# PSUM banks for layer-one sums and transposed rows, the place of the transposes, and a search level of ten VectorE operations

## The chip, the core and the metric

The kernel runs on one core of a Trainium2 chip. Times are device microseconds of the whole program. Before the change three runs took 708.53, 710.94 and 711.21 us, median 710.94. A separate execution, recorded by the hardware profiler, took 707.02 us; its span from the first to the last instruction is 705.3 us.

In what follows PE is TensorE, PEld its weight load, DVE is VectorE, ACT ScalarE, POOL GpSimd and SP the engine that issues most transfers.

## What is computed

Two stages. First a retention attention: for 8 batches, 8 heads, 576 positions and 64 features, scores times a decay mask times v. Its output is 4608 tokens of 512 features. Then a mixture of 8 experts, in which each expert takes exactly 576 tokens:

```python
logits = x @ w_gate                     # 4608 x 8
for idx in np.argsort(-logits.flatten()):
    tok, e = idx // 8, idx % 8
    if assigned[tok] >= 0 or counts[e] >= 576: continue
    assigned[tok] = e; counts[e] += 1
for e in range(8):
    out[assigned == e] = np.maximum(x[assigned == e] @ w1[e], 0) @ w2[e]   # 512 -> 1024 -> 512
```

The greedy assignment is not done token by token: the kernel searches for the score at which the next expert becomes full, removes that expert and its tokens, and searches again.

## The kernel before

The attention fills about the first 180 us; the search for the first expert to fill runs to about 215 us. From there the experts run one after the other on PE, in the order in which they fill, called e = 0 to 7 here. For each, five indirect transfers on POOL (`gather`, L949) fetch its tokens into `xg`. `transposes` (L954 to 970) turns them on PE in five pieces j = 0 to 4, four of 128 tokens and one of 64, each into one PSUM bank `pt`; ACT copies the bank to `xh` (the rounded high part) and DVE subtracts to get `xl` (the low part). `l1` (L972) forms 16 sums `ph`, one for each of eight blocks f of 128 hidden features and each of two token groups s (256 and 320 tokens): 12 matmuls into one bank, then ACT's ReLU into `hb` (L997) and DVE's low part of it (L1000). Both read the bank and thereby free it. `l2` (L1015) forms five sums `py` for five token pieces t, 24 matmuls for t = 0 to 3 and 16 for t = 4; ACT (for t = 4 also DVE, L1052) moves each to `yt`, and POOL scatters it to the output (L1009). `conv` (L923) splits a loaded weight piece `raw` into high and low parts with two ACT copies and a POOL accumulating transfer.

PSUM's eight banks are named by tag: "t" and "r" have one each, "y", "h0" and "h1" two each. A tag's buffers are taken in rotation, and an instruction that takes a buffer waits until its last readers are done. Before, `ph` with s = 0 always took "h0" and with s = 1 "h1", so a sum had to wait for the readers of the sum two blocks earlier. `py` has "y". The five pieces of a transpose took t, h0, h1, t, h0 for e of 1 and above, and t, y, y, t, y for e = 0. Everything of the search uses "r".

While PE works for expert e, DVE searches for a later expert (`search`, L285): seven levels. In a level DVE compares every token's candidate digit with K candidates (`reach`, L161, output `G`), PE counts with nine small matmuls into bank r (L312), and DVE turns the 32 x 8 counts into a digit `j` by twelve operations (L315 to L329). From it come `v` (L297), the next `G`, and `u` (L307). After the levels come `members` (PE at L383), `listing` (PE at L421 and L424) and `leave`, which takes the found expert out of the scores (`best`) and prepares the next search.

Every engine executes its instructions in the order in which the program emitted them. That order comes from a planner, `Mixer` (L854). It keeps an estimated PE time `t` and DVE time `v`; each matmul group of `l1` or `l2` advances `t` (`mix.adv`), and DVE work beside the search advances `v` (`mix.vec`). The search is a generator that yields an estimated DVE duration and PE duration; its next piece is emitted when `t` reaches the time at which the estimate says it is ready. A gather notes when its rows will have come, as `t` plus a constant (`arrives`, L952), and the transposes begin at the first slot of `l2` after that, one piece a slot. The estimates are constants in the code and know nothing of real waits.

Of the kernel before, what the change touches and what calls it, by code (L numbers as in the profile page):

```python
# [10 lines left out]
F32 = mybir.dt.float32  # L11
# [3 lines left out]
ALU = mybir.AluOpType  # L15
AF = mybir.ActivationFunctionType
AX = mybir.AxisListType
# [46 lines left out]
def widths(shifts):  # L64
    return [1 << (a - b) for a, b in zip([32] + shifts[:-1], shifts)]
# [16 lines left out]
class Route:  # L82
# [202 lines left out]
    def search(s):  # L285
        nc, V, pool, ps = s.nc, s.nc.vector, s.pool, s.ps
        SH, KK = LATER, widths(LATER)
        for _ in s.ordered():
            pass
        s.dig(0)  # L290
        for it, K in enumerate(KK):
            last = it == len(SH) - 1
            v2 = pool.tile([128, 36, 2], BF16, name="v", bufs=2)
            v = v2[:, :, 0]
            if it:

                V.tensor_scalar(v2, u[:, :, None].to_broadcast([128, 36, 2]), j, None, op0=ALU.subtract)  # L297
            else:
                V.tensor_copy(v2, s.dg[:, 0, :, None].to_broadcast([128, 36, 2]))
            s.reach(0, 36, K, v2, ALU.is_le)  # L300
            if it == 0:
                for k in range(1, 7):
                    s.dig(k)
                V.tensor_copy(s.D[:, 1:], s.dg[:, 1:])
            if not last:
                u = pool.tile([128, 36], F32, name="u")
                V.scalar_tensor_tensor(u, v, float(KK[it+1]), s.D[:, it+1], op0=ALU.mult, op1=ALU.add)  # L307

            yield (2050 + 19*K if it else 1350), 310
            cp = ps.tile([128, 32], F32, name="r")  # L310
            for c in range(0, 36, 4):
                nc.tensor.matmul(cp, s.G[:, c:c+4].rearrange("p c k -> p (c k)"), s.oh[:, c:c+4, :], start=(c == 0), stop=(c == 32))  # L312
            own = [cp[32*c:32*c+32, 8*c:8*c+8] for c in range(4)]
            cs, ct = pool.tile([32, 8], F32, name="cs"), pool.tile([32, 8], F32, name="ct4")
            V.tensor_tensor(cs, own[0], s.nr[:32], op=ALU.add)  # L315
            V.tensor_copy(ct, own[1])
            V.tensor_tensor(cs, own[2], cs, op=ALU.add)
            V.tensor_tensor(ct, own[3], ct, op=ALU.add)
            V.tensor_tensor(cs, cs, ct, op=ALU.add)
            if last:  # L320
                break

            mc, mq = pool.tile([32, 1], F32, name="mc"), pool.tile([128, 1], F32, name="mq")
            tc, j = pool.tile([128, 32], F32, name="tc"), pool.tile([128, 1], F32, name="j")
            V.tensor_reduce(mc, cs, axis=AX.X, op=ALU.max)
            for q in range(0, 128, 32):
                V.tensor_scalar(mq[q:q+32], mc, 0.0, float(KK[it+1]), op0=ALU.is_ge, op1=ALU.mult)  # L327
            V.transpose(tc, mq.to_broadcast([128, 32]))
            V.tensor_reduce(j, tc[:, 1:K], axis=AX.X, op=ALU.add)  # L329

        for q in range(0, 128, 32):
            V.tensor_scalar(s.f[q:q+32, :8], cs, 0.0, None, op0=ALU.is_ge)
        tf, cf = pool.tile([128, 32], F32, name="tc"), pool.tile([128, 32], F32, name="cf")
        nk, nf = pool.tile([128, 1], F32, name="nk"), pool.tile([128, 1], F32, name="nf")
        w = pool.tile([128, 8], F32, name="w8")
        s.ge = pool.tile([128, 2, 36], F32, name="ge")
        s.gt, s.eq = s.ge[:, 0], s.ge[:, 1]
        V.transpose(tf, s.f)
        V.tensor_reduce(nk, tf[:, :K], axis=AX.X, op=ALU.add)
        V.transpose(cf, nk.to_broadcast([128, 32]))  # L340
        V.tensor_reduce(nf, cf[:, :8], axis=AX.X, op=ALU.max)
        V.scalar_tensor_tensor(w, cf[:, :8], nf, s.dec, op0=ALU.is_equal, op1=ALU.mult)
        V.tensor_scalar(s.gt, v, nf, -1.0, op0=ALU.subtract, op1=ALU.is_gt)
        V.tensor_scalar(s.eq, v, nf, -1.0, op0=ALU.subtract, op1=ALU.is_equal)
        s.pick(w)
# [539 lines left out]
def moe(tc, nc, P, R, xd, w1_d, w2_d, out, mix):  # L885
    V, A, T = nc.vector, nc.scalar, nc.tensor
# [4 lines left out]
    state = dict(dma=0, conv=0, most=2, listing=-1)  # L891
# [51 lines left out]
    def gather(e):  # L943
        if e in XG or not ready(e):
            return
        xg = P["c"].tile([128, 5, DM], F32, name="xg", tag="xg")
        for j in range(5):
            n = 128 if j < 4 else 64
            nc.gpsimd.indirect_dma_start(out=xg[:n, j, :], out_offset=None, in_=xd[:, :],  # L949
                                         in_offset=bass.IndirectOffsetOnAxis(ap=found[e][:n, j:j+1], axis=0))  # L950
        XG[e] = xg
        state['arrives'] = mix.t + 7000  # L952

    def transposes(e):  # L954

        xg = XG[e]
        xh = P['w'].tile([128, 4, 576], F32R, name="xh", bufs=1)
        xl = P['w'].tile([128, 4, 576], F32R, name="xl", bufs=1)
        XH[e], XL[e] = xh, xl
        for j in range(5):  # L960
            n = 128 if j < 4 else 64
            tag = ("t", "h0", "h1")[j % 3] if e else ("t", "y", "y")[j % 3]
            pt = P['ps'].tile([128, 4, 128], F32R, name="pt", tag=tag, bufs=1 + (tag != "t"))
            for d in range(4):
                T.transpose(pt[:, d, :n], xg[:n, j, d*128:(d+1)*128].bitcast(F32R), P['ident_r'][:n, :n])  # L965
            o, l = [x[:, :, j*128:j*128+n] for x in (xh, xl)]
            A.activation(o, pt[:, :, :n].bitcast(F32), AF.Copy)
            V.tensor_tensor(l, pt[:, :, :n].bitcast(F32), o.bitcast(F32), op=ALU.subtract)
            mix.vec(610)
            yield  # L970

    def l1(e, tr):  # L972
# [5 lines left out]
        for i, (f, s) in enumerate(order):  # L978
# [6 lines left out]
                    pass  # L985
            xh, xl = XH[e], XL[e]
            c, n = ((slice(0, 256), 256), (slice(256, 576), 320))[s]
            ps = P['ps'].tile([128, n], F32, name="ph", tag=f"h{s}", bufs=2)
            terms = [(w[:, d], x[:, d, c]) for d in range(4) for w, x in ((wh, xh), (wh, xl), (wl, xh))]
            if e == 0 and f < 2:  # L990
                terms = terms[0::3] + terms[2::3] + terms[1::3]
# [6 lines left out]
            for a, b in ((0, 256),) if s == 0 else ((0, 256), (256, 320)):  # L998
                to = (640 if a == 0 else 64) + 256*s
                V.scalar_tensor_tensor(hb[:, f, to+a:to+b], ps[:, a:b], 0.0, hb[:, f, 256*s+a:256*s+b].bitcast(F32),  # L1000
                                       op0=ALU.max, op1=ALU.subtract)
# [13 lines left out]
    def l2(e, hb):  # L1015
# [42 lines left out]
        if e + 1 < E and e + 1 not in XH:  # L1058
            mix.drain(lambda: ready(e + 1))
            gather(e + 1)  # L1060
            tr = transposes(e + 1)
# [88 lines left out]
```

## Time and profile before

| What | Value |
|---|---|
| Runs | 708.53, 710.94, 711.21 us; median 710.94 |
| Profiled execution | 707.02 us, its span 705.3 us |
| Mean granted PE clock | 0.984 |
| PE busy over the span | 664.8 us, 94% |
| DVE, ACT, POOL busy | 434.5, 315.5, 182.8 us |
| 228 to 545 us (experts, with searches) | PE busy 300.14 of 317 us, DVE 256.82 |
| 545 to 672 us (experts, no search left) | PE busy 127.00 of 127 us, DVE 30.61 |

The profiled execution lies 3.9 us under the median of the runs. An instruction's row shows its start, its duration, and in brackets how long its engine had stood idle before it and whose end ended that. Matmuls overlap: one row is longer than the distance to the next, so idle time in front of a matmul is counted from the modelled end of the one before, and is a little less than what the stream lost.

### The profile page before, as it was taken

What the parts mean: (1) busy time and instruction counts of PE and PEld (TensorE: products, weight loads), DVE (VectorE), ACT (ScalarE), POOL (GpSimd) and SP (SyncE); (2) the same over time, 40 slices, a digit from 0 to 9 for tenths busy, and PEclk for the clock granted to TensorE, in tenths of its full rate; (3) what the DMA queues carried; (4) which work ended last, traced back from release to release, by engine and by line L of the source; (5) the groups of instructions that cost most, each with busy time, mean ns of one, the idle gap of its engine ahead of it and who ended that gap; (6) DMA issues with size and microseconds to landing.
All of it is one profiled execution on the core that took longest, in us unless ns stands there. A gap on an engine that the chain in (4) does not pass through costs nothing.

```text
span 705.3 us, 14450 instructions
## 1 busy us (share of the span) xinstructions
PE 664.8 (94%) x5462; PEld 579.3 (82%) x5464; DVE 434.5 (62%) x1656; ACT 315.5 (45%) x551; POOL 182.8 (26%) x236
## 2 busy tenths in 40 slices
PE   5999999999899989999999998999999999999995
PEld 5998988879684877798688778778978988988984
DVE  4466766857846588989688788769977321321200
ACT  2655555545311733455345514633551671571511
POOL 3222211121203211614314314124123233232111
PEclk9999999999959999999999999999999999999999
DMA  7986688785316664987938946884794796895421
GB/s 226 348 303 232 218 275 304 244 278 155 101 66 232 146 152 131 229 214 227 253 90 227 227 126 168 205 208 125 179 229 135 184 220 199 204 219 176 90 60 37
DMA packets 53429, 134.74 MB, mean 191 GB/s; under 512 B 6128, under 2 KB 22512, under 8 KB 53360
## 3 DMA queue, kind: packets, MB, share of 16 engines
q1 hardware_dynamic: 38400, 81.91, 34.6%
q0 software_dynamic: 14960, 51.91, 33.2%
q8 instruction: 43, 0.70, 0.4%
q14 instruction: 26, 0.21, 0.1%
HBM read 81.90 MB, written 18.87 MB: 143 GB/s over the span
## 4 chain that ended last, share of the span: by engine, by line
PE 59%; DVE 20%; DMA 8%; issue 6%; ACT 3%; SPq 1%; POOL 1%; POOLq 0%; DVEq 0%; ACTq 0%
PE py L1032 20%; PE ph L993 15%; PE pA L577 7%; PE pX L628 4%; DMA raw<-in_w 3%; PE pS L593 3%; PE pX L618 3%; DVE hb L1000 2%; DVE G L161 2%; PE pt L965 1%; DVE mq L327 1%; PE r L270 1%; DMA vin<-in_vk 1%; PE pT L657 1%; DMA w1l<-raw 1%
## 5 line engine op out<-in xcount | busy, mean ns | idle before, releaser
L1032 PE MATMUL py<-w2h,hb 128*128 128x512 f32 x576 | 189.1, 401 | 0.0
L993 PE MATMUL ph<-xh,w1h 128*128 128x320 f32 (+1 forms) x512 | 152.6, 302 | 4.7 <-DVE hb L1000 2.5
L993 PE MATMUL ph<-xh,w1l 128*128 128x320 f32 (+1 forms) x512 | 149.6, 296 | 0.5 <-DMA w1l<-raw 0.5
L993 PE MATMUL ph<-xl,w1h 128*128 128x320 f32 (+1 forms) x512 | 149.5, 296 | 0.0
L1032 PE MATMUL py<-w2l,hb 128*128 128x512 f32 (+1 forms) x320 | 125.8, 393 | 0.0
L1032 PEld LDWEIGHTS py<-w2h,hb 128*128 128x128 f32 x576 | 104.6, 189 | 21.1
L993 PEld LDWEIGHTS ph<-xh,w1h 128*128 128x128 f32 x512 | 96.3, 189 | 6.8 <-ACT w2l L937 2.6
L997 ACT ACTIVATE hb<-ph 128x256 fp32r<-128x256 f32 (+1 forms) x128 | 52.0, 408 | 109.8 <-PE ph L993 107.6
L993 PEld LDWEIGHTS ph<-xh,w1l 128*128 128x128 f32 x512 | 96.3, 189 | 0.7 <-DMA w1l<-raw 0.7
L993 PEld LDWEIGHTS ph<-xl,w1h 128*128 128x128 f32 x512 | 96.5, 190 | 0.3
L1000 DVE SCALAR_TENSOR_TENSOR hb<-ph,hb 128x256 fp32r<-128x256 f32 (+1 forms) x192 | 58.8, 352 | 54.7 <-ACT hb L997 54.1
L577 PE MATMUL pA<-qin,kz 128*128 128x128 f32 x576 | 75.5, 287 | 7.2 <-DMA qin<-in_qk 5.8
L599 ACT ACTIVATE S<-pS,cst 64x128 f32<-64x128 f32 x128 | 46.4, 362 | 76.5 <-PE pS L593 74.9
L577 PEld LDWEIGHTS pA<-qin,kz 128*128 128x128 f32 x576 | 70.3, 200 | 9.7 <-ACT kz L518 7.6
L1009 POOL DMA_INDIRECT out_y<-yt,idx x40 | 40.3, 1008 | 114.4 <-ACT yt L1049 75.7
L1032 PEld LDWEIGHTS py<-w2l,hb 128*128 128x128 f32 (+1 forms) x320 | 57.0, 178 | 13.3 <-DMA w2l<-raw 0.2
L559 POOL TENSOR_TENSOR ks<-nin,cst 128x512 f32<-128x512 f32 (+1 forms) x33 | 33.4, 1028 | 131.1 <-DMA nin<-in_vk 67.9
L1049 ACT ACTIVATE yt<-py 128x512 f32<-128x512 f32 x32 | 19.1, 598 | 104.1 <-PE py L1032 81.4
L581 DVE TENSOR_TENSOR am<-pA,cst 128x512 f32<-128x512 f32 (+1 forms) x80 | 48.3, 633 | 24.1 <-PE pA L577 23.8
L938 POOL DMA_DIRECT2D w2l<-raw x32 | 28.8, 899 | 127.3 <-ACT hb L997 127.3
L949 POOL DMA_INDIRECT xg<-xd,idx x40 | 41.0, 1025 | 67.6 <-issue 30.0
L1052 DVE TENSOR_TENSOR yt<-yt,py 64x512 f32<-64x512 f32 x8 | 5.4, 680 | 69.7 <-ACT yt L1051 69.6
(179 smaller groups left out, 985.6 us busy)
## 6 DMA issues: line engine op xcount, KB each, us to landing
raw<-in_w SPq DMA_DIRECT2D x64, 512.0 KB, 5.2
w2l<-raw POOLq DMA_DIRECT2D x32, 512.0 KB, 5.1
w1l<-raw POOLq DMA_DIRECT2D x31, 512.0 KB, 6.0
kin<-in_qk SPq DMA_DIRECT2D x14, 576.0 KB, 6.5
qin<-in_qk SPq DMA_DIRECT2D x14, 576.0 KB, 7.0
vin<-in_vk SPq DMA_DIRECT2D x14, 576.0 KB, 5.7
nin<-in_vk SPq DMA_DIRECT2D x14, 512.0 KB, 5.3
xd<-xr SPq DMA_DIRECT2D x36, 192.0 KB, 3.1
```

The lines of the kernel that those rows point to most:

```text
L559: nc.gpsimd.tensor_tensor(KS[u][:, a:b], LD[u, 'n'].rearrange("p (a d) -> p a d", d=64)[:, a:b], ks[:, u % HP, a:b, None].to_broadcast([12 ...
L577: nc.tensor.matmul(pa[:, j, h], KZ[u % 2][:, h, s], LD[u, 'q'][:, s], start=True, stop=True)
L581: nc.vector.tensor_tensor(am[:, :n], pa[:, :n], m[:, None, 2*hp:2*hp+2, :].to_broadcast([128, n, 2, 128]), op=ALU.mult)
L599: nc.scalar.activation(st[64*h:64*h+64, :, 64*h:64*h+64], PS[u][64*h:64*h+64], AF.Copy, scale=ss[64*h:64*h+64, hp, c:c+1])
L628: nc.tensor.matmul(px[64*h:64*h+64, :], v[:, blk*128+64*h:blk*128+64*h+64], AM[g][:, h, :], start=False, stop=blk < 8, skip_group_check=True)
L938: nc.gpsimd.dma_start(lo, raw, accum_op=ALU.add)
L949: nc.gpsimd.indirect_dma_start(out=xg[:n, j, :], out_offset=None, in_=xd[:, :], in_offset=bass.IndirectOffsetOnAxis(ap=found[e][:n, j:j+1] ...
L993: T.matmul(ps, w, x, start=(k == 0), stop=(k == 11))
L997: A.activation(hb[:, f, c], ps, AF.Relu)
L1000: V.scalar_tensor_tensor(hb[:, f, to+a:to+b], ps[:, a:b], 0.0, hb[:, f, 256*s+a:256*s+b].bitcast(F32), op0=ALU.max, op1=ALU.subtract)
L1009: st = nc.gpsimd.indirect_dma_start(out=out[:, :], out_offset=bass.IndirectOffsetOnAxis(ap=found[e][:n, t:t+1], axis=0), in_=y[:n], in_off ...
L1032: T.matmul(ps[:m], a, w, start=(k == 0), stop=(k == last), skip_group_check=True)
```

## The change

Line numbers here are those of the kernel before; in the changed kernel they are one or two lower or higher in these functions.

- `l1`: the sums of the blocks f = 2 and f = 5 take their bank from "y" and no longer from h0 or h1.
- `transposes`: for e of 1 and above the pieces take t, h0, h1, h0, h1. For e = 0 the list is spelled out and is the same as before.
- `gather`: `arrives` is the planned time plus 9000 in place of 7000.
- `search`: the counts are summed with reversed sign by three operations in a row, the last of the four count blocks is compared with that sum in four operations that write the 128 x 8 array `f` directly, and one reduction over `f` takes the place of the reduction and the four 32 x 1 comparisons. The factor K moves from there into `v` (a second operation of the same instruction), and `D` is divided by K once for each search so that `u` is a plain sum. The planner's numbers for a level are kept.

```diff
-                V.tensor_scalar(v2, u[:, :, None].to_broadcast([128, 36, 2]), j, None, op0=ALU.subtract)
+                V.tensor_scalar(v2, u[:, :, None].to_broadcast([128, 36, 2]), j, float(K), op0=ALU.subtract, op1=ALU.mult)
...
-                V.tensor_copy(s.D[:, 1:], s.dg[:, 1:])
+                for a, b in ((1, 4), (4, 7)):
+                    V.tensor_scalar(s.D[:, a:b], s.dg[:, a:b], 1.0/KK[a], None, op0=ALU.mult)
...
-                V.scalar_tensor_tensor(u, v, float(KK[it+1]), s.D[:, it+1], op0=ALU.mult, op1=ALU.add)
+                V.tensor_tensor(u, v, s.D[:, it+1], op=ALU.add)
...
-            cs, ct = pool.tile([32, 8], F32, name="cs"), pool.tile([32, 8], F32, name="ct4")
-            V.tensor_tensor(cs, own[0], s.nr[:32], op=ALU.add)
-            V.tensor_copy(ct, own[1])
-            V.tensor_tensor(cs, own[2], cs, op=ALU.add)
-            V.tensor_tensor(ct, own[3], ct, op=ALU.add)
-            V.tensor_tensor(cs, cs, ct, op=ALU.add)
+            cs = pool.tile([32, 8], F32, name="cs")
+            V.scalar_tensor_tensor(cs, s.nr[:32], -1.0, own[0], op0=ALU.mult, op1=ALU.subtract)
+            for x in own[1:3]:
+                V.tensor_tensor(cs, cs, x, op=ALU.subtract)
+            for q in range(0, 128, 32):
+                V.tensor_tensor(s.f[q:q+32, :8], own[3], cs, op=ALU.is_ge)
...
-            V.tensor_reduce(mc, cs, axis=AX.X, op=ALU.max)
-            for q in range(0, 128, 32):
-                V.tensor_scalar(mq[q:q+32], mc, 0.0, float(KK[it+1]), op0=ALU.is_ge, op1=ALU.mult)
+            V.tensor_reduce(mq, s.f[:, :8], axis=AX.X, op=ALU.max)
...
-        for q in range(0, 128, 32):
-            V.tensor_scalar(s.f[q:q+32, :8], cs, 0.0, None, op0=ALU.is_ge)
...
-        state['arrives'] = mix.t + 7000
+        state['arrives'] = mix.t + 9000
...
-            tag = ("t", "h0", "h1")[j % 3] if e else ("t", "y", "y")[j % 3]
+            tag = ("t", "h0", "h1", "h0", "h1")[j] if e else ("t", "y", "y", "t", "y")[j]
...
-            ps = P['ps'].tile([128, n], F32, name="ph", tag=f"h{s}", bufs=2)
+            ps = P['ps'].tile([128, n], F32, name="ph", tag="y" if f in (2, 5) else f"h{s}", bufs=2)
```

How the rows move on the engines is shown at three places. Everything up to the first search level inside `l1` of e = 0 stands as before on PE, and POOL's rows are the same throughout.

DVE, one level of the search in `l1` of e = 0 (`cs`, `ct`, `mc`, `mq`, `tc`, `j` are the small tiles between the counts `r` and the digit `j`). Before:

```order
L315 TENSOR_TENSOR cs<-r,room 32x8
L316 COPY ct_2952<-r 32x8
L317 TENSOR_TENSOR cs<-r,cs 32x8
L318 TENSOR_TENSOR ct_2952<-r,ct_2952 32x8
L319 TENSOR_TENSOR cs<-cs,ct_2952 32x8
L325 TENSOR_REDUCE mc<-cs 32x1
L327 TENSOR_SCALAR mq<-mc 32x1 x4
L328 STREAM_TRANSPOSE tc<-mq 128x32
L329 TENSOR_REDUCE j<-tc 128x1
L297 TENSOR_SCALAR v<-u,j 128x72
L161 TENSOR_TENSOR G<-ct,v 128x1152
L307 SCALAR_TENSOR_TENSOR u<-v,D 128x36
```

Now:

```order
L317 SCALAR_TENSOR_TENSOR cs<-room,r 32x8
L319 TENSOR_TENSOR cs<-cs,r 32x8 x2
L321 TENSOR_TENSOR f<-r,cs 32x8 x4
L327 TENSOR_REDUCE mq<-f 128x1
L328 STREAM_TRANSPOSE tc<-mq 128x32
L329 TENSOR_REDUCE j<-tc 128x1
L297 TENSOR_SCALAR v<-u,j 128x72
L161 TENSOR_TENSOR G<-ct,v 128x1152
L308 TENSOR_TENSOR u<-v,D 128x36
```

Twelve operations between the counts and `j` have become ten, and seven of them instead of four read the counts' bank.

ACT, from the third `yt` of e = 0's `l2` to the first ReLU of e = 1's `l1` (`w1h`, `w1l` are a `conv`, `xh` the transposed pieces). Before:

```order
L1049 ACTIVATE yt<-py 128x512
L967 ACTIVATE xh<-pt 128x4x128
L933 ACTIVATE w1h<-raw 128x1024
L937 ACTIVATE w1l<-raw 128x1024
L967 ACTIVATE xh<-pt 128x4x128 x3
L1049 ACTIVATE yt<-py 128x512
L967 ACTIVATE xh<-pt 128x4x64
L933 ACTIVATE w1h<-raw 128x1024
L937 ACTIVATE w1l<-raw 128x1024
L1051 ACTIVATE yt<-py 64x512
L997 ACTIVATE hb<-ph 128x256
```

Now:

```order
L1048 ACTIVATE yt<-py 128x512
L931 ACTIVATE w1h<-raw 128x1024
L935 ACTIVATE w1l<-raw 128x1024
L965 ACTIVATE xh<-pt 128x4x128
L1048 ACTIVATE yt<-py 128x512
L965 ACTIVATE xh<-pt 128x4x128 x3
L931 ACTIVATE w1h<-raw 128x1024
L935 ACTIVATE w1l<-raw 128x1024
L965 ACTIVATE xh<-pt 128x4x64
L1050 ACTIVATE yt<-py 64x512
L996 ACTIVATE hb<-ph 128x256
```

Four of the five pieces now stand behind the fourth `yt`, and the last one behind the fourth `conv` as well.

PE, in the same `l2` after the first nine small matmuls of a search. Before:

```order
L1032 MATMUL py<-w2h,hb 128x512 x2
L1032 MATMUL py<-w2l,hb 128x512
L1032 MATMUL py<-w2h,hb 128x512 x2
L1032 MATMUL py<-w2l,hb 128x512
L965 MATMUL pt<-ident,xg 128x128 x4
L1032 MATMUL py<-w2h,hb 128x512 x2
L1032 MATMUL py<-w2l,hb 128x512
L965 MATMUL pt<-ident,xg 128x128 x4
```

Now:

```order
L1031 MATMUL py<-w2l,hb 128x512
L1031 MATMUL py<-w2h,hb 128x512 x2
L1031 MATMUL py<-w2l,hb 128x512
L963 MATMUL pt<-ident,xg 128x128 x4
L1031 MATMUL py<-w2h,hb 128x512
L1031 MATMUL py<-w2l,hb 64x512
L313 LDWEIGHTS G
L313 MATMUL r<-oh,G 128x32
```

The first piece stands after 15 `py` matmuls instead of 6, at the end of t = 3, and the other four within t = 4.

In `l2` of e = 1 the first piece stands behind 51 instead of 42 matmuls of `py`, in e = 2 behind 6 instead of 3; from e = 3 on it stands behind the first three, as before. The search's groups shift a little with them. Between L424 and the first group of L312 of the next search there now stand 66 matmuls of `ph` in e = 2, 63 in e = 3, and 54 with 2 of `py` in e = 4, where there stood 54 with 6 of `py` and 4 of `pt`, 69, and 63. On SP one weight load has changed places with the load of an expert's number.

More of the change, by code (lines that the diff above doesn't have):

```diff
@@ L313, in search @@
             own = [cp[32*c:32*c+32, 8*c:8*c+8] for c in range(4)]
-            cs, ct = pool.tile([32, 8], F32, name="cs"), pool.tile([32, 8], F32, name="ct4")
[L315 to L319, printed above, removed]
+            cs = pool.tile([32, 8], F32, name="cs")
[4 more added lines that the diff above has]
+                V.tensor_tensor(s.f[q:q+32, :8], own[3], cs, op=ALU.is_ge)
             if last:
                 break
-            mc, mq = pool.tile([32, 1], F32, name="mc"), pool.tile([128, 1], F32, name="mq")
+            mq = pool.tile([128, 1], F32, name="mq")
             tc, j = pool.tile([128, 32], F32, name="tc"), pool.tile([128, 1], F32, name="j")
-            V.tensor_reduce(mc, cs, axis=AX.X, op=ALU.max)
-            for q in range(0, 128, 32):
-                V.tensor_scalar(mq[q:q+32], mc, 0.0, float(KK[it+1]), op0=ALU.is_ge, op1=ALU.mult)
+            V.tensor_reduce(mq, s.f[:, :8], axis=AX.X, op=ALU.max)
             V.transpose(tc, mq.to_broadcast([128, 32]))
             V.tensor_reduce(j, tc[:, 1:K], axis=AX.X, op=ALU.add)
-        for q in range(0, 128, 32):
-            V.tensor_scalar(s.f[q:q+32, :8], cs, 0.0, None, op0=ALU.is_ge)
         tf, cf = pool.tile([128, 32], F32, name="tc"), pool.tile([128, 32], F32, name="cf")
```

## Prediction

> **What bounds the kernel now.** I read the stages first, then PE's waits in the stage that has them, then the single waits in the order of time.
>
> The stages (from the view by windows; columns: stretch, its length, busy us and instructions of PE, PEld, DVE, ACT, POOL, then PE clock, DMA share, GB/s):
>
> ```profile
> core 0: us, PE busy (x) PEld busy (x) DVE busy (x) ACT busy (x) POOL busy (x), PEclk, DMA share, GB/s
> 228.00:545.00 317.00, 300.14 (x2135) 259.30 (x2134) 256.82 (x1142) 142.35 (x223) 92.91 (x120) 0.99 0.71 182
> 545.00:672.00 127.00, 127.00 (x803) 115.95 (x802) 30.61 (x88) 65.42 (x104) 35.20 (x49) 1.00 0.73 182
> ```
>
> Once no search is left (545 to 672 us) PE is never idle. While searches run beside the experts it is idle for 16.9 of 317 us, at full clock and with the transfers at the same 0.7 share in both. What differs is DVE: 257 us busy against 31. The diff leaves the attention and the search for the first expert as they are. So the question is which of these 16.9 us go. The view of waits, PE alone, 228 to 545 us (us in total, times, longest):
>
> ```profile
> PE r L312 <- DVE G L161: 5.8, 8, 2.0
> PE pt L965 <- DVE xl L968: 4.1, 4, 1.7
> PE ph L993 <- DVE hb L1000: 2.5, 3, 1.1
> PE ph L993 <- ACT hb L997: 1.2, 1, 1.2
> PE r L383 <- DVE sc L374: 0.9, 1, 0.9
> PE ph L993 <- ACT xh L967: 0.9, 1, 0.9
> PE ph L993 <- DMA w1l<-raw: 0.5, 1, 0.5
> PE r L421 <- DVE rh L415: 0.5, 1, 0.5
> ```
>
> They add to 16.4 us. The 0.9 on xh and the 0.5 on w1l are the first expert's start, which the diff does not touch. 15.0 us are left, of three kinds: banks that DVE or ACT free late (4.1 + 2.5 + 1.2 = 7.8), search levels that DVE finishes late (5.8), and the two steps after the search (1.4). The largest ones, from the timeline of PE (start, us, idle before and whose end it waited for):
>
> ```profile
> 250.24 0.39 PE L312 MATMUL r<-oh,G 128*128 128x32 bf16 x9 [1.95 <-DVE G L161]
> 284.05 0.39 PE L312 MATMUL r<-oh,G 128*128 128x32 bf16 x9 [1.16 <-DVE G L161]
> 336.04 0.40 PE L1032 MATMUL py<-w2l,hb 128*128 128x512 f32 x1
> 338.18 0.54 PE L965 MATMUL pt<-ident,xg 128*128 128x128 f32 x4 [1.74 <-DVE xl L968]
> 382.87 0.38 PE L993 MATMUL ph<-xh,w1h 128*128 128x320 f32 x1 [1.09 <-DVE hb L1000]
> 414.51 0.39 PE L312 MATMUL r<-oh,G 128*128 128x32 bf16 x9 [0.68 <-DVE G L161]
> 425.33 0.38 PE L993 MATMUL ph<-xh,w1h 128*128 128x320 f32 x1 [1.20 <-ACT hb L997]
> 433.83 0.39 PE L993 MATMUL ph<-xh,w1h 128*128 128x320 f32 x1 [1.09 <-DVE hb L1000]
> ```
>
> And the normal pace, from the chain of waits:
>
> ```profile
> 544.93 20.99 PE ph L993 x156
> 571.29 22.29 PE py L1032 x97
> ```
>
> So a ph matmul takes 20.99/156 = 0.135 us and a py matmul 22.29/97 = 0.23. At 338.18 the start lies 2.14 us behind the one before, 1.91 more than 0.23, while the row says 1.74 idle: each wait costs the stream about 0.17 us beyond its row.
>
> **The change, part by part.**
>
> **Transposed rows (4.1 us).** At 338.18 the fourth piece wants bank t, which the first piece holds until DVE's subtraction; DVE does a whole search level first. With five different banks no piece waits for another. The two h0 and two h1 banks were last read for the blocks f = 6 and 7, one expert's l1 earlier; the pieces come at least 3 py matmuls apart, and DVE's reads of those blocks run ahead of the xl work in its queue. I take all 4.1; the bound on the other side is that the last piece waits for f = 7's readers, and half comes back.
>
> **Banks of the first layer (3.7 us).** A sum's bank came free when the readers of the sum two blocks earlier were done. With f = 2 and 5 in y every bank comes back after three blocks: one block is 24 matmuls, 24 x 0.135 = 3.2 us more cover, against waits of 1.2 at most. All 3.7 go. Part returns, since PE now reaches the next search sooner and DVE does not. The case after 425.33, from PE's and DVE's timelines:
>
> ```profile
> 426.96 0.17 PE L424 MATMUL r<-n,ones 128*128 128x8 bf16 x1
> 435.62 0.76 DVE L161 TENSOR_TENSOR G<-ct,v 128x1152 bf16<-128x1152 bf16 x1
> 437.55 0.39 PE L312 MATMUL r<-oh,G 128*128 128x32 bf16 x9
> ```
>
> DVE's G ends at 436.38, 9.4 us behind L424. PE now has 63 ph matmuls between the two, 63 x 0.135 + 0.2 = 8.7 us: a new wait of 0.7. In e = 2 the 66 matmuls (9.1 us) give 0.3 by the same 9.4. In e = 4 PE had 63 matmuls (8.7 us) and no wait in the list; with 54 ph and 2 py (7.9 us) and less hb work for DVE I estimate 0.3. That is 1.3 us against the 7.8; the ends are 0 and 3.7.
>
> **Search levels.** From the groups of instructions (busy us, mean ns of one | idle before):
>
> ```profile
> L315 DVE TENSOR_TENSOR cs<-r,room 32x8 f32<-32x8 f32 x42 | 6.2, 147 | 20.6 <-PE r L312 20.5
> L316 DVE COPY ct<-r 32x8 f32<-32x8 f32 x42 | 6.6, 156 | 1.3
> L317 DVE TENSOR_TENSOR cs<-r,cs 32x8 f32<-32x8 f32 x42 | 6.7, 160 | 1.3
> L318 DVE TENSOR_TENSOR ct<-r,ct 32x8 f32<-32x8 f32 x42 | 7.0, 167 | 1.3
> L319 DVE TENSOR_TENSOR cs<-cs,ct 32x8 f32<-32x8 f32 x42 | 6.5, 154 | 1.4
> L325 DVE TENSOR_REDUCE mc<-cs 32x1 f32<-32x8 f32 x36 | 5.4, 149 | 1.2
> L327 DVE TENSOR_SCALAR mq<-mc 32x1 f32<-32x1 f32 x144 | 20.8, 144 | 2.7
> L332 DVE TENSOR_SCALAR f<-cs 32x8 f32<-32x8 f32 x24 | 4.0, 166 | 0.5
> L351 DVE TENSOR_REDUCE mx<-w 128x1 f32<-128x8 f32 x8 | 1.3, 157 | 0.0
> L433 DVE TENSOR_TENSOR lo<-r,lo 32x40 f32<-32x40 f32 x14 | 2.8, 197 | 0.4
> ```
>
> Removed from a level: 147 + 156 + 160 + 167 + 154 + 149 + 4 x 144 = 1509 ns. Added: three sums at 160, four comparisons at 166 (nearest rows L318 and L332, same size), a reduction at 157: 1301 ns. That is 208 less, and two gaps of 30 ns (1.3 us/42) less: 0.27 us a level. The trace shows no comparison of this kind; were it 144 as for L327, the saving would be 0.36, were it 197 (a read of counts five times as wide, L433), 0.15. The last level loses 784 + 4 x 166 = 1448 and gains 480 + 664: 0.30, with two gaps 0.36 us. The second operation in v and the plain sum for u I cost at nothing: L297 and L307 keep their shape, and both run while DVE waits for PE anyway (20.5 us idle before L315). The division of D by K is two instructions for one, after G, in the same cover; without cover six times 0.2 to 0.3 us.
>
> The Trainium skill speaks against this. VectorE: DVE Perf Modes, "The TRN2 errata", gives a VectorE instruction a fixed cost of 58 cycles with operands in SBUF and 120 from PSUM, at 0.96 GHz. By it the four comparisons rise from about 61 ns to 133 each and a level becomes some 0.08 us longer. This trace does not agree: L317 reads PSUM at 160 ns, L319 SBUF alone at 154.
>
> Of the eight waits on G the two at 250.24 and 284.05 make 3.1. The second is the first level of a search, with no level ahead of it, and stays; the first loses 0.27. Of the other six (together 2.7 us, between 0.2 and 0.7 each) each loses up to 0.27, about 1.5. I take 1.8 of the 5.8. The waits at L383 and L421 follow the last level; 0.36 each, as far as it goes: 0.7 of 1.4.
>
> **Transposes later in the plan.** The waits on gathered rows are not in the list above, so the two more microseconds remove none. In l2 of e = 0 they cost. ACT's, PE's and DVE's rows there, from the timeline:
>
> ```profile
> 291.82 0.60 ACT L1049 ACTIVATE yt<-py 128x512 f32<-128x512 f32 x1 [1.29 <-DMA out_y<-yt,idx]
> 292.31 0.38 ACT L967 ACTIVATE xh<-pt 128x256 fp32r<-128x256 f32 x1
> 292.57 1.06 ACT L933 ACTIVATE w1h<-raw 128x1024 fp32r<-128x1024 f32 x1
> 293.52 1.06 ACT L937 ACTIVATE w1l<-raw 128x1024 fp32r<-128x1024 f32 x1
> 296.12 0.31 PE L993 MATMUL ph<-xh,w1h 128*128 128x320 f32 x1
> 295.25 0.68 DVE L1052 TENSOR_TENSOR yt<-yt,py 64x512 f32<-64x512 f32 x1 [0.23 <-ACT yt L1051]
> ```
>
> ACT's fourth yt waits until 291.82 for a scatter to free its tile; POOL's order is unchanged, so this stays. Behind it now stand three pieces of xh (0.49 apart as these rows, 1.5 us), a conv (2.0 us from 292.57 on) and the last piece (0.38): 291.82 + 0.49 + 1.5 + 2.0 + 0.38 = 296.2, and DVE's xl, by estimate, 0.4 later. PE wants xh at 296.12 less what it no longer waits in this l2, about 295.7. I take a new wait of 0.7 us; ends 0 (the scatter lands sooner) and 3 (the conv's weights are late too). In e = 1 and 2 the pieces are still 40 and more matmuls ahead of their use. SP's swapped load already waits for a buffer.
>
> **Sum**, against the profiled execution: -4.1 - 3.7 + 1.3 - 1.8 - 0.7 + 0.7 = -8.3; the eight bank waits and two small ones on G that vanish take 10 x 0.17 along, -1.7: **-10.0 us**. Span 705.3 to 695.3, own time 707.0 to 697.0. The profiled execution lay 3.9 under the median, so I apply the difference to the median: 710.9 - 10.0 = **700.9 us**. Bounds of the terms: the hand-back (0 to 3.7), the levels (0.15 to 0.36), the new wait (0 to 3) and half of 4.1 give 695 to 707 at the extremes together, 698 to 705 as the likely part.
>
> **Rivals.**
>
> *DVE sets the pace.* Whatever PE gains at a bank it loses at the next G. For it: DVE is busy 81% of the stage. Against it: it still sits idle 20.5 us waiting for PE's counts. Then only the levels' own saving remains, 1.8 + 0.7 + 0.5 = 3.0: 707.9 us.
>
> *DVE gets ahead.* Every level being 0.27 shorter, the slack adds up from level to level; the waits on G vanish but for the one at 284.05, and so do the hand-back and the new wait: 10.0 + 2.8 + 1.3 + 0.7 = 14.8 less, 696.1. Against it: PE's groups are placed by planned time, and slack beyond the place is not used.
>
> *The comparisons are dear.* Reading PSUM four times more at 197 ns: 0.12 less saving a level, the level terms shrink by about 1.4: 702.3. The small gap between L317 and L319 speaks against it. The Trainium skill's page named above (VectorE: DVE Perf Modes) has the same mechanism.
>
> *Slower: the y banks.* The sums of f = 2 now wait until ACT and DVE have read the last two py. ACT's yt can be held by a scatter, as at 291.82. f = 2 begins 48 matmuls, 6.5 us, into l1, and the second sum 1.4 later. If the last yt came 2 us after that in all seven later experts, 14 us would be added to -10.0: 715. It decides from 13.6/7 = 1.9 us on. Against it: in e = 1, where the scatter held ACT, DVE's read (L1052 above) ended at 295.93, before even the second sum of l1 began at 296.12.
>
> **Chances.** The forecast 0.62, DVE ahead 0.13, DVE's pace 0.13, dear comparisons 0.06, slower 0.06. A difference under 0.5% (3.6 us, 707.4) can't be told from none here. Faster: 0.62 + 0.13 + 0.06 and a quarter of the pace case: 0.84; within 0.5%: 0.10; slower: 0.06. Range 695.5 to 708, from the case with DVE ahead to that where it sets the pace; the forecast's own is 698 to 705.
>
> **What would show it.** In the profile of the changed kernel between 228 and 545 us: no wait of pt on xl, none of ph on hb; four comparisons at 150 to 170 ns each and a level 0.27 us shorter; the waits on G near 4 to 5 us, with new ones behind L424 in e = 3 and 4; a wait of ph on xh or xl at about 296 us; everything after the last search 10 us earlier and otherwise the same. A G total above 9 us would mean that DVE sets the pace; a wait of ph on yt would mean the y banks.

## The result, and the profile after

The changed kernel takes **698.47 us** (median of six runs, 697.27 to 700.15). The kernel before took 709.37 beside it (six runs, 706.55 to 711.21). The ratio is 0.9845, 95% interval 0.9818 to 0.9871: 1.5% faster, 10.9 us, where 10.0 and 700.9 us were forecast. The profiled execution took 698.68 us, its span 696.9. Of the executions behind the tables further down, one of the kernel with the layer's banks alone (806.47 us) and one of the kernel before on that chip (2196.69 us) lie far above all others, and the ratios leave them out.

The stages of the changed kernel, by the view by windows (columns as in the prediction). The searches now end earlier, so the first stretch ends at 538 us:

```profile
228.00:538.00 310.00, 299.55 (x2146) 261.56 (x2145) 247.50 (x1073) 142.38 (x223) 93.81 (x120) 0.99 0.73 186
538.00:663.00 125.00, 124.95 (x786) 113.58 (x785) 28.03 (x77) 64.79 (x103) 35.03 (x47) 1.00 0.75 185
```

PE is idle for 10.45 of 310 us. In the kernel before the same stretch of time reads:

```profile
228.00:538.00 310.00, 294.07 (x2086) 253.52 (x2085) 250.68 (x1119) 140.56 (x219) 89.62 (x117) 0.99 0.73 185
```

That was 15.93 idle. From the first `ph` to the last instruction the profile shortens from 476.7 us (228.6 to 705.3) to 468.5 (228.4 to 696.9), 8.2 of the 8.4 us between the two spans. The gain lies in the stretch with searches: behind the last search PE is as full as it was. PE's waits in the changed kernel, 228 to 538 us (us in total, times, longest):

```profile
PE r L313 <- DVE G L161: 6.8, 7, 2.2
PE ph L992 <- issue: 1.0, 1, 1.0
PE ph L992 <- ACT xh L965: 0.9, 1, 0.9
PE ph L992 <- DMA w1l<-raw: 0.6, 1, 0.6
PE r L381 <- DVE sc L372: 0.4, 1, 0.4
PE r L313 <- issue: 0.3, 1, 0.3
```

Both kinds of bank wait are gone: no pt on xl (4.1 before), no ph on hb (2.5 + 1.2). What is left is DVE's G, and it has grown from 5.8 to 6.8. The longest single waits, from PE's timeline:

```profile
250.35 0.39 PE L313 MATMUL r<-oh,G 128*128 128x32 bf16 x9 [2.20 <-DVE G L161]
284.20 0.39 PE L313 MATMUL r<-oh,G 128*128 128x32 bf16 x9 [1.15 <-DVE G L161]
428.11 0.39 PE L313 MATMUL r<-oh,G 128*128 128x32 bf16 x9 [0.30 <-issue]
477.58 0.39 PE L313 MATMUL r<-oh,G 128*128 128x32 bf16 x9 [1.07 <-DVE G L161]
484.03 0.31 PE L992 MATMUL ph<-xl,w1h 128*128 128x320 f32 x1 [1.02 <-issue]
490.17 0.39 PE L313 MATMUL r<-oh,G 128*128 128x32 bf16 x9 [1.61 <-DVE G L161]
```

The rows at 284.20, 428.11 and 477.58 are first levels of a search, behind L422 (L424 before). The last two are new: this is the hand-back that was forecast, PE reaching the next search sooner than DVE.

The longest wait, at 250.35, is the third level of the first of these searches. It was 1.95 before and was to lose 0.27. The level itself is shorter, 3.02 us from its first operation to the end of G where it was 3.30. But DVE begins it only after a low part of `hb`, and ACT makes that `hb` only after a conv, for which it waits for a weight piece to land:

```profile
244.62 1.06 ACT L931 ACTIVATE w2h<-raw 128x1024 fp32r<-128x1024 f32 x1 [2.28 <-DMA raw<-in_w]
246.93 0.42 DVE L999 SCALAR_TENSOR_TENSOR hb<-ph,hb 128x256 fp32r<-128x256 f32 x1 [3.21 <-ACT hb L996]
```

That conv began at 244.24 before, 0.38 us earlier, so the later landing took back what the shorter level gained. At 484.03 PE stands for a microsecond with no wait that the profile shows, and at the next level, 490.17, it waits 1.61 for DVE.

The forecast new wait is at its place. ACT's rows, and then PE's:

```profile
291.80 0.60 ACT L1048 ACTIVATE yt<-py 128x512 f32<-128x512 f32 x1 [2.77 <-DMA out_y<-yt,idx]
292.30 1.57 ACT L965 ACTIVATE xh<-pt 128x512 fp32r<-128x512 f32 x3
293.73 1.09 ACT L931 ACTIVATE w1h<-raw 128x1024 fp32r<-128x1024 f32 x1
294.68 1.08 ACT L935 ACTIVATE w1l<-raw 128x1024 fp32r<-128x1024 f32 x1
295.63 0.41 ACT L965 ACTIVATE xh<-pt 128x256 fp32r<-128x256 f32 x1
```

```profile
295.67 0.28 PE L992 MATMUL ph<-xh,w1l 128*128 128x256 f32 x1
296.09 0.41 PE L992 MATMUL ph<-xh,w1h 128*128 128x320 f32 x1
296.55 0.41 PE L992 MATMUL ph<-xl,w1h 128*128 128x320 f32 x1
```

The two starts lie 0.42 and 0.46 behind the one before them, where the pace of their shapes is 0.12 and 0.15: 0.6 us lost (0.7 forecast).

DVE's level, from the groups of instructions (busy us, mean ns of one | idle before):

```profile
L321 DVE TENSOR_TENSOR f<-r,cs 32x8 f32<-32x8 f32 x168 | 28.4, 169 | 3.1
L319 DVE TENSOR_TENSOR cs<-cs,r 32x8 f32<-32x8 f32 x84 | 13.0, 155 | 2.9
L317 DVE SCALAR_TENSOR_TENSOR cs<-room,r 32x8 f32<-32x8 f32 x42 | 6.1, 144 | 19.7 <-PE r L313 18.4 <-PE py L1031 1.1
L327 DVE TENSOR_REDUCE mq<-f 128x1 f32<-128x8 f32 x36 | 5.8, 162 | 1.2
```

144 + 2 x 155 + 4 x 169 + 162 = 1292 ns where 1301 were forecast, for 1509 removed: with two gaps of 30 ns 0.28 us a level.

### The profile page after: what moved, and what is told of

Its sections match the earlier page's. It is cut to its first block, busy times and chain, and to the rows that moved or that the text cites. A ratio compares the mean times of both kernels' runs of the same rounds, so it can differ in the third digit from the quotient of the medians.

```text
span 696.9 us, 14355 instructions
## 1 busy us (share of the span) xinstructions
PE 663.6 (95%) x5462; PEld 580.5 (83%) x5464; DVE 423.6 (61%) x1578; ACT 316.1 (45%) x551; POOL 183.8 (26%) x236
## 4 chain that ended last, share of the span: by engine, by line
PE 74%; DVE 11%; DMA 5%; issue 5%; ACT 3%; SPq 1%; POOL 1%; POOLq 0%; DVEq 0%; ACTq 0%
PE ph L992 23%; PE py L1031 23%; PE pA L575 8%; PE pX L626 4%; PE pS L591 3%; PE pX L616 3%; PE pt L963 2%; DMA raw<-in_w 2%; PE r L313 2%; DMA nin<-in_vk 1%; PE pT L655 1%; PE r L270 1%; DVE G L161 1%; PE pX L614 1%; PE pT L695 1%
```

## The experiments

Eight kernels take the parts one by one: four undo one part in the changed kernel, four put one part alone into the kernel before. Four more follow what these left open. Kernels that are compared ran on one chip beside the kernel before, which took 710.18 us on the chip of the parts alone and 705.65 on that of all the others. Theory A is the prediction's sum, theory B that DVE hands gains back.

**One part undone.** In the changed kernel:

```diff
# u_banks
-            ... tag="y" if f in (2, 5) else f"h{s}", bufs=2)
+            ... tag=f"h{s}", bufs=2)
# u_rows
-            tag = ("t", "h0", "h1", "h0", "h1")[j] if e else ("t", "y", "y", "t", "y")[j]
+            tag = ("t", "h0", "h1")[j % 3] if e else ("t", "y", "y")[j % 3]
# u_plan
-        state['arrives'] = mix.t + 9000
+        state['arrives'] = mix.t + 7000
# u_search: the twelve operations of a level, v, u and D as in the kernel before
```

> The changed kernel with one part undone: all sums of layer one take h0 or h1 again. Theory A (the waits add up): waits of ph on hb come back, 3 to 4 us in all, part of them taken off the waits on G; time about 2 to 4 us over the changed kernel's 698.5, that is 700.5 to 702.5. Theory B (VectorE sets the pace, a wait removed at a bank reappears at the next G): ph waits come back but the waits on G fall by as much, time within 1 us of 698.5.

> The changed kernel with the transposed rows in banks t, h0, h1, t, h0 again. Theory A: pt waits for xl again, some 4 us, time 702 to 703. Theory B: the same waits, but no G wait behind them as large as before, time within 1 us of 698.5.

> The changed kernel with the old search level of twelve operations. Theory A: no waits at the banks, waits on G some 2 to 3 us above the changed kernel's 6.8, time about 701.5. Theory B: a level longer by 0.27 us in each of 42 levels shows almost whole, 8 us or more: 706 or above.

> The changed kernel with the planned arrival of the rows at 7000 again. Theory A: the wait of ph on xh and xl near 296 us (0.6 us start to start) goes, the search groups stand where they stood before, time within 1.5 us of 698.5 on either side. Rival: the later transposes are themselves what gains, time 701.5 or above.

Measured, with the changed kernel itself on the same chip (called the repeat; its own section is below):

| Kernel | us | ratio to before, 95% | against the changed kernel | PE's waits, us |
|---|---|---|---|---|
| changed kernel (the repeat) | 695.23 | 0.9858 (0.9831 to 0.9885) | | 7.0 |
| banks of layer 1 undone | 697.46 | 0.9890 (0.9866 to 0.9914) | +2.2 | 9.5 |
| rows' banks undone | 697.49 | 0.9884 (0.9862 to 0.9906) | +2.3 | 8.2 |
| search levels undone | 695.44 | 0.9862 (0.9838 to 0.9885) | +0.2 | 9.5 |
| place of transposes undone | 695.72 | 0.9872 (0.9849 to 0.9894) | +0.5 | 7.6 |

The difference to the changed kernel is one of medians, uncertain by about 2.6 us (two ratios, each within 0.0022 to 0.0027), so none of the four is told from nothing by itself. Together they make 5.2, where the medians of the kernel before and the changed kernel lie 10.4 apart. Theory B's 8 us or more for the search levels did not come, nor the rival's 3 for the place of the transposes. Theory A's 2 to 4 for the layer's banks fits; its 4 for the rows' banks and 3 for the levels are more than was measured. The last column adds up PE's waits in each profile, from the first `ph` to the end of the last search. It is one execution each: the first profile of the changed kernel had 10.0 where the repeat has 7.0.

With the rows' banks undone there are three banks again, and of the 4.1 us on xl only 0.6 come back, in one wait. With the layer's banks undone 1.9 us of ph on hb return, about half of what the kernel before had.

**One part alone.** The same edits, the other way round, in the kernel before.

> The kernel before with one part alone: the sums of f = 2 and 5 in y. Theory A: no wait of ph on hb, waits on G a little larger, about 3 us less than the kernel before (709.4): 706.5. Theory B: the waits move to G, time within 1 us of 709.4.

> The kernel before with the transposed rows in five different banks alone. Theory A: no wait of pt on xl, 4 us less: 705.5. Theory B: within 1 us of 709.4.

> The kernel before with the shorter search level alone. Theory A: about 3 us less (706.5), the waits at the banks a little smaller but there. Theory B: 8 us or more less (701 or below).

> The kernel before with the planned arrival at 9000 alone. Theory A: waits of pt on xl stay near 4 us, a new wait of ph on xh near 296 us of 0.6 us, time within 1.5 us of 709.4. Rival (the later transposes gain by themselves): 3 us or more less.

| Kernel | us | ratio to before, 95% | PE's waits, us (16.4 before) |
|---|---|---|---|
| layer's banks alone | 708.39 | 0.9981 (0.9956 to 1.0007) | 16.8 |
| rows' banks alone | 700.82 | 0.9878 (0.9847 to 0.9908) | 13.5 |
| search levels alone | 705.78 | 0.9958 (0.9931 to 0.9984) | 15.6 |
| place of transposes alone | 703.56 | 0.9915 (0.9887 to 0.9944) | 14.6 |

By these ratios the four would make 1.3 + 8.7 + 3.0 + 6.0 = 19.0 us; the whole makes 10.9. By the waits they make 5.1 (-0.4, 2.9, 0.8 and 1.8), and the whole 9.4 in the repeat. The layer's banks alone gain nothing that can be told. PE's waits there (228 to 545 us):

```profile
PE r L312 <- DVE G L161: 7.1, 7, 2.1
PE pt L965 <- DVE xl L968: 5.0, 4, 2.5
...
PE pt L965 <- DVE cs L315: 0.9, 1, 0.9
PE pt L965 <- ACT w1h L933: 0.5, 1, 0.5
```

The waits on hb are gone, and 1.3 more at G, 0.9 more at xl and two new ones of 1.4 have taken their place: 3.6 of 3.7 handed back, as theory B had it. The search levels alone give the 3.0 that the prediction's pace case had for them (1.8 + 0.7 + 0.5).

The surprise is the place of the transposes, which the prediction gave a loss. Its waits of pt on xl (228 to 545 us):

```profile
PE pt L965 <- DVE xl L968: 0.8, 2, 0.5
```

They were 4.1 and have all but gone, with the three old banks. The rows of the wait at 338.18 show how. In the kernel before, PE and then DVE:

```profile
332.79 0.39 PE L312 MATMUL r<-oh,G 128*128 128x32 bf16 x9
333.03 0.52 PE L965 MATMUL pt<-ident,xg 128*128 128x128 f32 x4
...
338.18 0.54 PE L965 MATMUL pt<-ident,xg 128*128 128x128 f32 x4 [1.74 <-DVE xl L968]
336.53 0.76 DVE L161 TENSOR_TENSOR G<-ct,v 128x1152 bf16<-128x1152 bf16 x1
337.43 2.65 DVE L968 TENSOR_TENSOR xl<-pt,xh 128x512 fp32r<-128x512 f32 x4
```

With the place of the transposes alone:

```profile
333.18 0.39 PE L312 MATMUL r<-oh,G 128*128 128x32 bf16 x9
335.56 0.45 PE L965 MATMUL pt<-ident,xg 128*128 128x128 f32 x4
...
339.08 0.54 PE L965 MATMUL pt<-ident,xg 128*128 128x128 f32 x4
337.43 0.76 DVE L161 TENSOR_TENSOR G<-ct,v 128x1152 bf16<-128x1152 bf16 x1
338.33 1.89 DVE L968 TENSOR_TENSOR xl<-pt,xh 128x512 fp32r<-128x512 f32 x3
```

The level's counts come at nearly the same time (332.79 and 333.18). Before, the first piece followed them at once and the fourth was wanted while DVE was still in that level. Two microseconds later the first piece comes 2.4 us behind the counts, and the fourth is wanted when the level is over and DVE has begun xl at 338.33. Same three banks, no wait.

Two times do not fit their waits. The rows' banks alone gain 8.7 us (6.5 to 10.8), and their waits are 2.9 less: the 4.1 of pt on xl are gone, and G has one more. The later place alone gains 6.0 (4.0 to 8.0), and its waits are 1.8 less: of the 3.3 at xl, 1.9 came back at G. The granted clock shows a second price of a wait. In the kernel before, a wait on xl that ends at 451.93, and then two stretches by the view by windows:

```profile
451.93 0.55 PE L965 MATMUL pt<-ident,xg 128*128 128x128 f32 x4 [1.68 <-DVE xl L968]
453.40:456.60 3.20, 3.20 (x11) 2.55 (x11) 0.86 (x2) 2.27 (x3) 0.18 (x1) 0.50 0.84 294
457.00:460.00 3.00, 3.00 (x22) 2.32 (x22) 1.94 (x13) 2.46 (x3) 1.35 (x3) 1.00 0.79 153
```

From 453.3 to 456.7 PE's clock is halved, and the starts of the py matmuls lie 0.42 to 0.51 us apart, where the pace is 0.23. By these rows that costs about 1.5 us, an estimate, and no idle time shows it. Of the fourteen profiles twelve have such stretches between the first `ph` and 680 us, seventeen in all. Each begins within about 2 us of the end of a wait of 1.1 to 4.4 us and lasts 3.4 us, only that of the search levels alone (behind 337.72) 6.8. The layer's banks alone have three, the later place alone two; the kernel before, the rows' banks alone and the changed kernel have one each; with the rows' banks or the place undone there is none. Not every wait of this length brings one: in the kernel before those that end at 250.24 (1.95 us) and 338.18 (1.74) did not. What decides it stays open.

With 1.5 us a stretch added to the list of waits, the time from the first `ph` to the last instruction follows in the profiles. The later place alone should be 1.8 - 1.5 = 0.3 shorter than the kernel before, and is (476.4 for 476.7); the place undone should be 0.6 - 1.5 = -0.9 beside the repeat, and is -1.1 (463.5 for 464.7).

The mean clock of each execution is on record, and the times go with it. On this chip 22 executions of the kernel before took 710.18 to 712.78 us where it was 0.978 or 0.979, and 705.03 to 708.15 where it was 0.985 to 0.988; one stretch takes about 3.4 x 0.5 / 705 = 0.0024 off it. All six of the rows' banks alone had 0.985 to 0.988. Their median lies 5.3 us under the 706.17 of the kernel before at the same clock, near 4.1 with 4 x 0.17. Three executions with the later place had 0.986, and their median of 703.42 lies 2.7 under the same 706.17. So a part of these gains is probably a halved clock that does not come; of the other executions no profile shows the stretches. On the other chip the whole gains 8.6 us at 0.986 (703.7 and 695.1, medians of four and of two executions) and 10.4 by all.

**Two parts undone together, and the changed kernel once more.** If the new banks of the rows and the later place each remove the same waits, undoing both must cost what neither did.

```diff
# u_rowsplan, in the changed kernel: both lines as in u_rows and u_plan
-            tag = ("t", "h0", "h1", "h0", "h1")[j] if e else ("t", "y", "y", "t", "y")[j]
+            tag = ("t", "h0", "h1")[j % 3] if e else ("t", "y", "y")[j % 3]
-        state['arrives'] = mix.t + 9000
+        state['arrives'] = mix.t + 7000
```

> The changed kernel once more, unaltered, so that the three kernels beside it have it on their own chip. All theories expect the ratio to the kernel before that it had: 0.9845, between 0.981 and 0.988; waits on G near 6.8 us, no wait of pt on xl, none of ph on hb.

> The changed kernel with two parts undone together: the transposed rows have their three old banks again (t, h0, h1, t, h0) and the transposes their old place in the plan (7 us after the gather, not 9). What stays is the new banks of the first layer and the short search levels. Theory of substitutes (each of the two removes the waits of pt on xl by itself, so that undoing one of them cost little): with both gone the waits come back whole, pt on xl 3 to 5 us, and the kernel is 6 to 7 us slower than the changed kernel, about 4 us faster than the kernel before (1.3 for the layer's banks and 3.0 for the levels, as they measured alone), ratio 0.993 to 0.995. Theory of the prediction's sum (rows' banks 4.1 and two waits' hidden 0.17 each, the later transposes -0.7): 4 us slower than the changed kernel, ratio about 0.990. Theory of a common pace (DVE hands back whatever is gained, so no part matters much): 0 to 2 us slower than the changed kernel, and the waits turn up as G instead of pt.

Both undone: 701.12 us, ratio 0.9938 (0.9917 to 0.9959); 5.9 us slower than the changed kernel, about 2.5 either way. That is near the 6 to 7 of the theory of substitutes, and more than the 2.3 + 0.5 of the two singly; by the time alone the 4 of the prediction's sum is not excluded. The waits speak for substitutes: pt on xl is 2.1 here, where it was 0.6 and none with one undone, and all of PE's waits rise by 3.9 (7.0 to 10.9), where singly they rose by 1.2 and 0.6. Pt on xl is back at half the size expected, with one wait on the gathered rows beside it:

```profile
PE pt L963 <- DVE xl L966: 2.1, 2, 1.1
...
PE pt L963 <- DMA xg<-xd,idx: 0.7, 1, 0.7
```

The two on xl stand at 337.82 and 446.63 us, where the two long ones of the kernel before stood (338.18 and 451.93). Behind the second the clock is halved. The list and this one more stretch make 3.9 + 1.5 = 5.4 us; from the first `ph` to the end the profile is 5.9 longer than the repeat (470.6 and 464.7).

The changed kernel itself: 695.23 us, ratio 0.9858, close to the 0.9845 of the first measurement, and all its waits in this stretch are

```profile
PE r L313 <- DVE G L161: 5.1, 7, 1.7
PE ph L992 <- ACT xh L965: 0.9, 1, 0.9
PE ph L992 <- DMA w1l<-raw: 0.6, 1, 0.6
PE r L381 <- DVE sc L372: 0.4, 1, 0.4
```

There is no issue wait, no wait at the level that stood at 490.17, and G is at 5.1: 1.7 at the level behind the weight piece (249.32 here), 2.5 at three first levels and 0.8 at three others. The fifth expert, from its first ph to that of the sixth, took 58.6 us here (468.1 to 526.7) against 61.5 (469.2 to 530.7) in the first profile: the stall at 484.03 and what followed it cost that execution 2.9 us and do not come in every execution of the kernel.

**Longer levels.** Is DVE's level a price that PE pays? Two idle additions more in each level, on numbers that nobody reads:

```diff
+            dm = pool.tile([32, 8], F32, name="dm")
+            for _ in range(2):
+                V.tensor_tensor(dm, s.nr[:32], s.nr[:32], op=ALU.add)
             for q in range(0, 128, 32):
                 V.tensor_tensor(s.f[q:q+32, :8], own[3], cs, op=ALU.is_ge)
```

> The changed kernel with two idle additions more on DVE in each of the 42 search levels (32x8, on numbers that nobody reads), between the subtractions and the comparisons: by the rows of its level 150 to 160 ns each and two gaps of 30 ns, about 0.37 us a level, 15.5 us in all. Theory A (only the levels whose counts PE reaches too early pay, some nine or ten, and a few join them): waits on G rise from 6.8 to 10 to 12 us and the kernel is 3 to 5 us slower than the changed kernel. Theory B (DVE's chain sets the pace of the stage with searches): 12 to 15 us slower, waits on G above 18 us. Theory C (the levels have slack by now, which is why the undone search part cost so little): 0 to 1 us slower.

696.72 us, ratio 0.9876 (0.9850 to 0.9902): 1.5 us above the changed kernel, within what can't be told apart. The added work:

```profile
L322 DVE TENSOR_TENSOR dm<-room 32x8 f32<-32x8 f32 x84 | 12.7, 151 | 1.4
```

84 additions with their gaps are 14.1 us of DVE; the waits on G rose from 5.1 to 6.6 us, all of PE's waits by 2.1 (7.0 to 9.1). About a seventh of it reached PE. Theory B falls (12 to 15 us, G above 18). Theory A's 10 to 12 at G did not come either, though its 3 us lies within the uncertainty of the time. Theory C, slack in most levels, is nearest. The undone search part says the same: it adds 0.28 x 42 = 11.8 us of DVE, and PE's waits rise by 2.5, a fifth. Its time rose by only 0.2, but in its profile the experts, from the first `ph` to the end, take 2.9 us longer than in the repeat (467.6 and 464.7), and they begin 1.6 us earlier (226.2 and 227.8).

**More room for the first levels.** 3.0 us of the waits that are left in the repeat of the changed kernel (1.16, 0.30 and 1.08, and what their starts lose beyond) stand at first levels of a search. A later place in the plan was to remove them:

```diff
-        state['arrives'] = mix.t + 9000
+        state['arrives'] = mix.t + 7000
...
-        yield (2400 if p == 0 else 3500), 0
+        yield (3700 if p == 0 else 4500), 0
```

> The changed kernel with the transposes back at 7 us in the plan, and the first level of each later search planned later: the planner's time for DVE behind the taking away of the chosen tokens is 3.7 us for 2.4 at the first search and 4.5 for 3.5 at the others, so that 78 ph matmuls (10.5 us) or more lie between L422 and that level, where DVE needs 9.4. Theory A (the waits at the first levels, 1.2 + 0.5 + 1.2 us and their hidden 0.17 each, are gone and no others come): waits on G 2 to 3.5 us, 2.5 to 4 us faster than the changed kernel, ratio about 0.980. Theory B (the whole search is one chain on DVE, a level placed later only moves its wait to the next level): waits on G as before, 5 to 7 us, time within 1 us of the changed kernel. Theory C (each search ends 1 us later than the one before it did, 6 us in the end, and gathered rows or weights come late): new waits of pt on xg or ph on w1h, 1 to 4 us slower.

704.41 us, ratio 1.0003 (0.9979 to 1.0027): 9.2 us slower than the changed kernel, all of its gain lost. PE's longest waits:

```profile
PE py L1031 <- DMA w2l<-raw: 6.1, 2, 4.4
PE ph L992 <- DVE xl L966: 4.1, 1, 4.1
PE r L313 <- DVE G L161: 1.8, 4, 1.0
```

Theory A was right on G (5.1 to 1.8) and theory C on the price, beyond its 1 to 4. The first loss, 4.1 us until 295.43, is the wait forecast for 296 us, grown: ACT, held by the scatter, has a whole conv and then four pieces of xh to do when it is let go.

```profile
291.68 0.60 ACT L1048 ACTIVATE yt<-py 128x512 f32<-128x512 f32 x1 [6.16 <-DMA out_y<-yt,idx]
292.17 1.05 ACT L931 ACTIVATE w1h<-raw 128x1024 fp32r<-128x1024 f32 x1
...
294.06 1.84 ACT L965 ACTIVATE xh<-pt 128x512 fp32r<-128x512 f32 x4
```

The second, 4.4 us until 333.52, runs through SP. The expert's number is read on SP (L899) when its search is done, and the loads of the running expert's weights stand behind that in SP's queue. In the repeat of the changed kernel the read after 300 us starts at 315.1, here at 322.9. Three loads of 512 KB then leave at 323.7, 324.3 and 324.9, and with them, at 323.88, the accumulating transfer of the last w2l, for which PE has no cover left. It landed 9.6 us after its issue; in the repeat the same transfer, issued at 320.7, took 5.1. That the shared transfer engines made it slow is read from the order of the rows and was not tried by itself. Behind both losses the clock is halved for 3.4 us: PE's waits rise by 7.2 (7.0 to 14.2), with one more stretch 8.7, and the profile is 9.0 longer from the first `ph` on (473.7 and 464.7).

## Why the prediction was right, and where its steps failed

**Right.** The stage and its bound: the gain is in the stretch with searches. The bank waits vanished, the hand-back came behind the same instruction, a new wait appeared at 296 us with 0.6 for 0.7, a level shortened by 0.28 for 0.27. The measured 698.5 lies inside the range (695.5 to 708), 2.4 under the forecast; 1.6 of that is the kernel before, which took 709.37 beside it and not 710.94.

**Failed: "the two more microseconds remove none".** The step looked only for waits on gathered rows. The place of the transposes also decides which search level DVE is in when the fourth piece wants its bank. Alone it took 3.3 of the 4.1 us on xl away and made the kernel faster, by 6.0 us in all executions and 2.7 at an equal clock. So the rows' banks and the later place are one term, not two: 2.3 and 0.5 undone singly, 5.9 together, in the waits 1.2, 0.6 and 3.9, where the prediction had 4.1 + 4 x 0.17 - 0.7, about 4, for both.

**Mis-sized: the layer's banks.** "All 3.7 go" holds, but with 1.3 handed back only when the other parts are there. Alone 3.6 of the 3.7 came back as waits at G and pt. In the whole, undoing them costs 2.2 of the 2.4 net; the uncertainty of 2.6 does not tell that from less.

**Mis-sized: the hand-back by place.** 0.46 us in e = 3 (0.7 forecast), 1.23 in e = 4 (0.3), none in e = 2 (0.3), counted as the delay of the start: 1.7 for 1.3 in all. The profile of the repeat shows the same two.

**Mis-sized: what a wait costs beyond its row.** The prediction had 0.17 us for each, taken from one start. Behind some waits a halved clock costs about 1.5 us more. So the price of a wait is not one number, and what the median of the kernel before had above its profiled execution (3.9 us) need not stay the same after the change, as the prediction took it to. Profile against profile the gain is 8.3 us, not 10.9.

**Near the forecast, with one step wrong: the search levels.** The saving a level is as forecast. Alone the levels are worth 3.0 us by the time, as the terms gave, and 0.8 by the waits; undone 0.2 by the time and 2.5 by the waits. These differ by no more than two executions of one kernel can, so the 3.0 is neither confirmed closely nor refuted. The step that failed is the wait at 250 us: it was 2.20 and then 1.75 where 1.95 less 0.27 was forecast, because it ends with the landing of a weight piece and not with a level's length. Of the 5.1 at G in the repeat 1.7 stands there and 2.5 at first levels, which have no shorter level ahead of them. The expectation of 4 to 5 at G does not follow from the terms either, which give 5.8 - 1.8 + 1.3 = 5.3; measured were 6.8 and 5.1.

**The rivals.** DVE's pace holds for the layer's banks alone, not for the whole: 14.1 us of added DVE work would have cost about as much. DVE ahead (696.1) did not come, since the first levels and the level behind the weight piece wait as they did. Dear comparisons: they took 169 ns against 155 for a sum of the same size, 14 ns each. An addition with operands in SBUF alone took 151, one that reads a sum from PSUM 155. The Trainium skill, VectorE: DVE Perf Modes, "The TRN2 errata", has 58 against 120 cycles for these, some 65 ns apart at its 0.96 GHz; these rows do not agree with that gap. The same section adds that its 58 is too low and that about 150 cycles were measured, by estimate 156 ns at that clock, which is near these rows. The y banks caused no wait: no row of ph on yt is in any of these lists.

**Why the sum came out right all the same.** The prediction priced each wait once, from the list of waits, and so could not count one twice; it failed in which part it gave a wait to. Without the row at 296 us and the 0.17 a wait, its terms take 9.0 off the list (4.1 + 3.7 - 1.3 + 1.8 + 0.7). The list fell from 16.4 us to 10.0 in the first profile and to 7.0 in the repeat, by 6.4 and 9.4. Beyond this it was partly luck: it counted no gain for the place of the transposes, the layer's banks by themselves give nothing, and a halved clock behind a wait has no term. That two parts remove the same waits is shown for the rows' banks and the later place; that all parts overlap is not.

## What to carry to other kernels

A wait on a bank behind an in-order engine depends on what that engine is doing when the bank is wanted: a bank more and a start two microseconds later can remove the same wait, so price the wait once and undo both edits together before calling either useless. A gain at one wait is kept only as far as the next in-order wait has slack; look there before adding terms. Before a search or any producer is planned later, follow what its result releases: here a register read in a load queue came 7.8 us later, and by the order of the rows that made transfers late that had nothing to do with the wait removed. A wait of a microsecond or two can cost as much again by a lower clock behind it, so look at the granted clock there, and compare executions of an equal clock before giving a part its price.

## What was not expected of the hardware

PE stood 1.02 us at 484.03 in one execution of the changed kernel with no wait that the profile shows, and not in its repeat, where that expert was 2.9 us shorter. With the place of the transposes alone it stood 0.26 and 0.41 us at 488.50 and 489.22, in the same expert and again just behind the counts of a search's second level, and there too a long wait on G followed (1.78 us at 495.62). No instruction was being loaded within 3 us of the first. What causes these stays open. The search levels alone also show 1.1 us put down to no wait, at 435.27, but that is at the sum which waited 1.09 for `hb` in the kernel before (433.83), so it is probably that bank wait.

A halved clock for 3.4 us behind a wait of 1.1 to 4.4 us, in twelve of fourteen profiles and not behind every such wait, had no term in the prediction; it is shown with the parts alone. The level of the times also differs by chip: the kernel before took 710.18 us on one and 705.65 on another, 0.6% apart, more than most parts of this change are worth, so that only kernels that ran on one chip were compared.
